# Sliding-window attention and a swish FFN on one core: two phases replaced by one planned graph of interleaved half batches

## The chip, the cores and the metric

The kernel runs on one core of a Trainium2 chip. The metric is the time of one execution on the device, in microseconds (us). Most executions of a kernel agree within about 1%. PE is the TensorE matmul engine, PEld its weight loads, DVE VectorE, ACT ScalarE, POOL GpSimd, SP the sync engine, whose queue issues most transfers. The "granted clock" is the share of PE's full speed that its throttle lets through. The traces record it only from 18 us on (before); the views count the unrecorded start as full clock. A run that is over 1.5% above the fastest of its kernel is called slow, and ratios use the other, fast runs alone.

## The reference

The inputs are float32. Attention with 4 sink tokens and a window of 128 is followed by a feed-forward network (FFN) with the activation h * sigmoid(beta * h).

```python
# q, k, v: (B=4, H=8, S=768, D=64); w_in (512, 2048); w_out (2048, 512); beta (2048,)
scores = q @ k.transpose(0, 1, 3, 2) / np.sqrt(D)
rel = pos[:, None] - pos[None, :]
keep = (pos[None, :] < 4) | ((rel >= 0) & (rel < 128))
a = softmax(np.where(keep, scores, -1e9))
x = (a @ v).transpose(0, 2, 1, 3).reshape(3072, 512)
h = x @ w_in
out = (h / (1 + np.exp(-beta * h))) @ w_out          # (3072, 512)
```

A block of 128 queries thus needs at most three blocks of 128 keys: its own (masked on the diagonal), the one before (masked the other way), and block 0, of which only the 4 sink keys count.

## The kernel before

There are two phases with a barrier between them. Phase A runs attention for the 16 pairs of heads, one pair after another. Each pair takes 12 transposes ahead of its scores, 30 score matmuls (contraction over 64 rows, the head dimension), six exps, six mask multiplications (two on GpSimd, four on DVE), and 30 AV matmuls. V carries a column of ones, so AV also gives the denominators. Every AV matmul contracts over 128 rows: for a sink block all 128 keys are multiplied, and the mask tile has set the exps of the other 124 to zero.

```python
# phase A, AV of one query block: all operands have 128 rows
lhsT = ET[:, e_idx, hh, j * 128:(j + 1) * 128]
rhs = v_aug[z][:, kb, hh, :]
te.matmul(out_ap, lhsT, rhs, start=(j == 0), stop=last)
...
# one pair after the other
for g in range(NPAIR):
    ...                                  # scores, exp, mask, AV of pair g
    epilogue_norm(g)
    transposes(g + 1)
    epilogue_trans(g)
    qk_copies(g + 1)
    epilogue_copy(g)
# phase B: 6 super-blocks of 512 tokens x 16 slices of d_ff
#   PE: 4 matmuls to hT (128x512); ACT: sig = sigmoid(beta * hT);
#   DVE: g = hT * sig; PE: 4 matmuls to the four output banks
```

The softmax here doesn't subtract the row's maximum and nothing guards it: scores larger than these inputs give would overflow.

## Time and profile before

The time is 329.79 us (median of three runs, 329.66 to 330.14).

| what | value | view |
|---|---|---|
| attention phase, up to the first FFN matmul | 153.6 us | timeline |
| mean granted clock there / afterwards | 0.66 / 0.99 | stretches |
| 128x512 matmul, start to start, full clock | 216 ns | matmul starts in the trace |
| 128-column transpose, start to start, half clock | 107 ns | same |
| one FFN super-block | 28.15 us | chain of waits |

First, lines of the page: busy time of each engine with its share of the span; then the span in 40 equal slices with the busy share in tenths (PEclk: granted clock in tenths).

```profile
PE 272.9 (83%) x2001; PEld 148.1 (45%) x2017; DVE 194.4 (59%) x329; ACT 141.2 (43%) x218; POOL 42.2 (13%) x52
...
PE   2577667766667688876999999999999999999994
...
PEclk9987576656775755575899999999999999999999
DMA  8999999999855576500000300030030002003003
```

Then the stretches before and after the first FFN matmul. The columns are the stretch, its length, busy time and number of instructions for PE, PEld, DVE, ACT and POOL, then granted clock, DMA share and GB/s.

```profile
0.00:153.60 153.60, 103.80 (x1250) 73.09 (x1251) 127.98 (x233) 63.14 (x98) 42.16 (x52) 0.66 0.79 179
153.60:329.00 175.40, 169.13 (x752) 75.06 (x766) 66.41 (x96) 78.09 (x121) 0.00 (x0) 0.99 0.10 37
```

The second phase is full of matmuls at full clock. In the first no engine is full: DVE is busiest (128 of 153.6 us), PE waits often and runs at half clock much of the time. The groups of instructions give the costs used below: line, engine, operation, tiles, shapes, count; busy us and mean ns of one; idle time just before, and what ended it.

```profile
L574 DVE TENSOR_TENSOR gsb<-hT,sig 128x512 bf16<-128x512 f32 x96 | 66.4, 692 | 103.9 <-PE oacc L595 92.0 <-ACT sig L566 11.9
L566 ACT ACTIVATE sig<-hT,beta_sb 128x512 bf16<-128x512 f32 x96 | 66.1, 689 | 92.8 <-PE hT L555 92.8
L354 PE MATMUL avout<-v_aug,ET 128*128 128x65 bf16 x480 | 40.9, 239 | 30.4 <-POOL ET L402 23.2 <-DVE ET L402 6.8
...
L393 ACT ACT_TABLE_LOAD x1 | 1.3, 1283 | 0.8 <-PEq L648 0.8
L566 ACT ACT_TABLE_LOAD x1 | 1.3, 1283 | 4.3 <-DVEq L500 4.3
```

The AV line (L354) gives a mean of 239 ns, which is the length of a pipelined matmul and not its cost. Its cost is the distance between starts, which is 54 ns here at half clock. The two table loads are one for exp and one for sigmoid.

### The profile page before, as it was taken

The numbers are of one execution on the slowest core, as the hardware profiler recorded it, in microseconds if no ns is written. First come the engines' busy times: TensorE is split into PE (matmuls) and PEld (weight loads), VectorE is DVE, ScalarE is ACT, GpSimd is POOL, SyncE is SP. The second block draws the span as 40 slices with busy tenths as digits, with TensorE's granted clock in tenths as the row PEclk, the third lists the DMA queues.
The fourth block names the chain that finished last, engine by engine and source line by source line (L and its number), as shares of the span: only waits on it lengthen the run. The fifth ranks groups of instructions, "written<-read, shape, count | busy, mean of one in ns | idle before, by whom it ended". The sixth has DMA issues, their size and how long they took to land.

```text
span 329.0 us, 5286 instructions
## 1 busy us (share of the span) xinstructions
PE 272.9 (83%) x2001; PEld 148.1 (45%) x2017; DVE 194.4 (59%) x329; ACT 141.2 (43%) x218; POOL 42.2 (13%) x52
## 2 busy tenths in 40 slices
PE   2577667766667688876999999999999999999994
PEld 1355445544444555553444444444444444444441
DVE  1687899999999999974344344334334334334331
ACT  1444443334444444443433633453453454445443
POOL 4222331123333222220000000000000000000000
PEclk9987576656775755575899999999999999999999
DMA  8999999999855576500000300030030002003003
GB/s 163 278 277 241 237 264 251 240 238 251 173 118 122 109 142 144 91 3 1 0 0 2 126 2 2 0 128 2 0 128 2 2 24 103 2 0 128 2 0 128
DMA packets 81465, 33.91 MB, mean 103 GB/s; under 512 B 75792, under 2 KB 75808, under 8 KB 80928
## 3 DMA queue, kind: packets, MB, share of 16 engines
q1 hardware_dynamic: 81440, 33.57, 41.8%
q8 instruction: 16, 0.26, 0.3%
q14 instruction: 9, 0.07, 0.1%
HBM read 27.27 MB, written 6.29 MB: 102 GB/s over the span
## 4 chain that ended last, share of the span: by engine, by line
PE 48%; issue 36%; POOL 10%; ACT 4%; DVE 1%; ACTq 0%; POOLq 0%; DVEq 0%
PE hT L555 24%; PE oacc L595 23%; POOL ET L402 9%; ACT outs L605 3%; POOL maskM L216 1%; ACT ET L393 1%; ACT sig L566 0%; DVE onorm L420 0%; PE avout L431 0%; PE avout L354 0%; DVE ET L402 0%; DVE xT L437 0%; ACTq L149 0%; POOL ident L216 0%; POOLq L50 0%
## 5 line engine op out<-in xcount | busy, mean ns | idle before, releaser
L574 DVE TENSOR_TENSOR gsb<-hT,sig 128x512 bf16<-128x512 f32 x96 | 66.4, 692 | 103.9 <-PE oacc L595 92.0
L566 ACT ACTIVATE sig<-hT,beta_sb 128x512 bf16<-128x512 f32 x96 | 66.1, 689 | 92.8 <-PE hT L555 92.8
L555 PE MATMUL hT<-xT,w_in 128*128 128x512 bf16 x376 | 99.5, 386 | 1.5 <-DVEq L500 1.1
L595 PE MATMUL oacc<-w_out,gsb 128*128 128x512 bf16 x376 | 99.0, 379 | 1.3
L393 ACT ACTIVATE ET<-score 128x768 bf16<-128x768 f32 (+1 forms) x96 | 61.5, 710 | 85.3 <-PE score L381 85.3
L354 PE MATMUL avout<-v_aug,ET 128*128 128x65 bf16 x480 | 40.9, 239 | 30.4 <-POOL ET L402 23.2
L595 PEld LDWEIGHTS oacc<-w_out,gsb 128*128 128x128 bf16 x384 | 37.5, 98 | 49.5 <-ACT outs L605 5.4
L555 PEld LDWEIGHTS hT<-xT,w_in 128*128 128x128 bf16 x384 | 38.1, 99 | 47.0 <-issue 2.8
L402 POOL TENSOR_TENSOR ET<-ET,maskM 128x256 bf16<-128x256 bf16 (+1 forms) x32 | 38.5, 1223 | 103.7 <-ACT ET L393 103.7
L354 PEld LDWEIGHTS avout<-v_aug,ET 128*128 128x128 bf16 x480 | 27.8, 122 | 47.0 <-POOL ET L402 30.0
L381 PE MATMUL score<-qkT 64*128 64x128 bf16 x480 | 31.8, 269 | 5.7 <-DVE qkT L322 3.2
L402 DVE TENSOR_TENSOR ET<-ET,maskM 128x768 bf16<-128x768 bf16 x64 | 32.1, 555 | 1.6 <-ACT ET L393 1.6
L381 PEld LDWEIGHTS score<-qkT 64*128 64x128 bf16 x480 | 17.9, 113 | 15.2 <-DVE qkT L322 8.4
L431 PE MATMUL avout<-ident,onorm 128*128 128x128 bf16 x96 | 12.2, 293 | 6.2 <-DVE onorm L420 6.2
L420 DVE TENSOR_TENSOR onorm<-avout,rden 128x384 bf16<-128x384 f32 x32 | 16.4, 552 | 0.6
L287 DVE CAST v_aug<-v_stage 128x768 bf16<-128x768 f32 x16 | 13.0, 814 | 3.6 <-DMA v_stage<-in_v_dram 3.6
L605 ACT ACTIVATE outs<-oacc 128x512 f32<-128x512 f32 x24 | 12.3, 604 | 1.4 <-PE oacc L595 1.4
L431 PEld LDWEIGHTS avout<-ident,onorm 128*128 128x128 bf16 x96 | 8.3, 130 | 10.3 <-DVE onorm L420 10.3
L437 DVE COPY xT<-avout 128x768 bf16<-128x768 bf16 x16 | 8.9, 556 | 0.9 <-PE avout L431 0.9
L320 DVE COPY qkT<-score 128x768 bf16<-128x768 bf16 x16 | 8.8, 548 | 0.0
L322 DVE COPY qkT<-score 128x768 bf16<-128x768 bf16 x16 | 8.8, 548 | 0.0
L409 DVE COPY den<-avout 128x12 f32<-128x12 f32 x16 | 2.7, 171 | 9.7 <-PE avout L354 9.7
(39 smaller groups left out, 99.9 us busy)
## 6 DMA issues: line engine op xcount, KB each, us to landing
q_stage<-in_q_dram SPq DMA_DIRECT2D x32, 192.0 KB, 4.6
k_stage<-in_k_dram SPq DMA_DIRECT2D x32, 192.0 KB, 4.9
v_stage<-in_v_dram SPq DMA_DIRECT2D x32, 192.0 KB, 4.1
out_dram<-outs SPq DMA_DIRECT2D x24, 256.0 KB, 2.3
w_in_stage<-in_moe_w_in_dram SPq DMA_DIRECT2D x4, 1024.0 KB, 6.8
w_out_stage<-in_moe_w_out_dram SPq DMA_DIRECT2D x4, 1024.0 KB, 7.5
beta_stage<-in_moe_beta_dram SPq DMA_DIRECT2D x1, 8.0 KB, 1.6
```

What stands on the lines that cost most here:

```text
L287: SD.op("dve", (lambda z: (lambda e: e.tensor_copy(v_aug[z][:, :, :, 0:D], v_stage[z][:, :, :, :])))(z), waits=[("vd%d" % z, 32 * nuse), ( ...
L354: (lambda te: te.matmul(out_ap, lhsT, rhs, start=(j == 0), stop=last)))
L381: (lambda te: te.matmul(out_ap, lhsT, rhs, start=True, stop=True)))
L393: (lambda e: e.activation(out_ap, in_ap, AF.Exp, bias=0.0, scale=SCALE)))
L402: (lambda e: e.tensor_tensor(out_ap, out_ap, mt, ALU.mult)))(out_ap, mt),
L420: (lambda e: e.tensor_tensor(dst, in0, in1, ALU.mult)))(dst, in0, in1),
L431: (lambda te: nc.tensor.transpose(out_ap, in_ap, ident[:, :])))(in_ap, out_ap),
L555: (lambda te: te.matmul(out_ap, lhsT, rhs, start=(c == 0), stop=last)))
L566: (lambda e: e.activation(sig_sb[i % NG][:, :], hT_ps[hb][:, 0:512], AF.Sigmoid, bias=0.0, scale=beta_sb[:, m:m + 1])))(i, m, hb),
L574: (lambda e: e.tensor_tensor(g_sb[i % NG][:, :], hT_ps[hb][:, 0:512], sig_sb[i % NG][:, :], ALU.mult)))(i, hb),
L595: (lambda te: te.matmul(out_ap, lhsT, rhs, start=(m == 0), stop=(m == NM - 1))))
L605: (lambda e: e.activation(out_sb[T % 2][:, t, :], out_acc[t][:, :], AF.Copy, bias=0.0, scale=1.0)))(T, t),
```

## The change

The intent is to fill PE's waits in attention with FFN matmuls, which have no dependence on the attention of later tokens. Everything becomes one graph. A planner in Python, with a small cost model, decides at build time in which order each engine gets its instructions; semaphores follow from the dependencies. The unit of attention is half a batch (3 query blocks) of one head pair. FFN super-blocks have 384 tokens, so that one needs just one half batch. Tanh replaces sigmoid: x*sigmoid(bx) = 0.5x(1 + tanh(bx/2)), the 0.5 folded into w_out. GpSimd masks each query block's own key block and the one before it with selects and does most casts of q, k and v. Of a sink block only the 4 sink keys are computed, as a 4-column score matmul and a 4-row AV matmul; so it needs no mask. (For the first two query blocks of a batch, block 0 is a window block too; it stays whole and is masked on DVE.)

The diff, cut to its core (removed phases and plumbing left out):

```diff
-        SD.op("act", ... e.activation(sig_sb[i % NG][:, :], hT_ps[hb][:, 0:512], AF.Sigmoid, ...
-        SD.op("dve", ... e.tensor_tensor(g_sb[i % NG][:, :], hT_ps[hb][:, 0:512], sig_sb[...], ALU.mult)
+        add("act", lambda e: e.activation(tt[ti][:, :], hp, AF.Tanh, bias=0.0, scale=hbeta[:, m:m + 1]), ...
+        add("dve", lambda e: e.scalar_tensor_tensor(gt[T_ % NG][:, m, :], tt[ti][:, :], 1.0, hp, ALU.add, ALU.mult), ...
...
+    GROUPS = [[[("s", 0, 0), ("s", 0, 1), ("d", 1, 1), ("p", 1, 2)], [("d", 2, 2), ("k", 0, 2)]],
+              [[("d", 3, 3), ("p", 2, 3), ("p", 3, 4)], [("d", 4, 4), ("d", 5, 5), ("p", 4, 5)],
+               [("k", 0, 3), ("k", 0, 4), ("k", 0, 5)]]]      # k: a sink block, 4 keys
...
+                dst = bank[0:NSINK if sink else 128, i0:i0 + st * (nq - 1) + 1:st, :]
+                lhsT = kt[rows, 1, 0:NSINK] if sink else kt[rows, 1, kc:kc + 128]
...
+                add("gp", ... e.affine_select(d, d, [[0, 2 * len(at_)], [sg, 128]], ALU.is_ge, 0.0, ...
...
+                    rows = slice(0, 128 if kb >= 0 else NSINK)          # AV
+                        e.matmul(A[:, c0:c0 + D + 1], E[z][rows, i, hh, :], vaug[vz][rows, kb % NK, 2 * hp + hh, :],
+                                 start=a, stop=o), mm_ns(D + 1), ...
...
+        for s in ("OT", "AV", "SC", "T") + ffn:     # planner: first head that is ready by now
+            h = head(s)
+            if h is None:
+                continue
+            if h[0] <= now:
+                best = (now, s, h[1])
+                break
```

## The prediction

> **What bounds the kernel now.** Two phases run one after the other. The timeline shows the first feed-forward (FFN) matmul at 153.6 us, after the last attention group. From there PE is the limit: the stretches from 160 us on are 98 to 99% PE at granted clock 1.00, the 128x512 matmuls start every 216 ns, a super-block takes 28.15 us. 768 x 216 ns = 166 us is that phase's floor; it takes about 175 us. The first 153 us are bound by no unit: one head pair takes 8 to 9.5 us in a serial loop. There DVE is 92% busy from 40 to 140 us, PE waits for GpSimd masks and DVE (the waits: 30.0 and 12.1 us), and the granted clock averages 0.66, so 128-column transposes start every 107 ns. The Trainium skill, "TensorE: Matmul & The Clock Gate", Part 1, says activity releases the half clock; the trace agrees (only 0.5 and 1.0 are granted; 1.0 throughout from 158 us).
>
> **What the change does.** FFN matmuls fill the attention's waits. PE work at full clock, from start-to-start times in the trace: FFN 166 us still (512 matmuls of 384 columns at about 162 ns, 384 of 512 at 216); transposes 288 x 56 ns = 16 us; scores: as many columns as before, the two heads' matmuls overlapping, about 14 us; AV 480 x about 42 ns = 20 us. Sum 216 us.
>
> Other engines, by estimate: ACT tanh 128 x 0.58 = 74 us, exp 65 us as before (61,440 columns), plus a share of copies; DVE g 128 x 0.56 = 71 us, normalisation 24 us, copies, masks and outputs 60 us, memsets 4 us. ACT and DVE together 300 us, 150 us each: below PE. GpSimd takes masks (about 55 us) and the q/k/v casts (about 41 us) at affine-select rates extrapolated from 292 ns for 128x128: about 100 us, off the limit, but it sets the pace of attention (13 us per half batch) until about 130 us. Tanh for sigmoid removes the second table load (1.28 us at 153.2 us): the skill's "ScalarE: Activation LUTs", Table sets, has exp and tanh in one set; the trace shows only that exp and sigmoid needed two.
>
> **Critical path.** Added to 216 us: the start. Half batch 0 (2.4 MB) lands by about 12 us, w_in by 28 us, half batch 1 by 37 us, w_out by 48 us at the 250 to 290 GB/s of the early slices; PE lacks work until then: about 35 us of work done at 50 us, so 15 us lost. Tail copy and store about 4 us. Waits where the planned order misjudges times, and half-clock windows while attention dominates: about 15 us, mostly before 130 us. Together 250 us.
>
> **Predicted: 250 us, 8 in 10 between 238 and 268 us. Faster by over 2%: 0.97, within 2%: 0.02, slower: 0.01.**
>
> **Right if:** one ACT table load; PE over 90% busy from 50 us to the end; granted clock 1.00 from 50 us but for a few windows; DMA input finished before about 130 us; ACT and DVE 55 to 70% busy, GpSimd 30 to 45%. Wrong if PE waits much on GpSimd masks, tanh or g.
>
> **What would make it wrong.** GpSimd selects slower than extrapolated (DVE colliding with it), so that attention stretches past 200 us; half clock persisting in the mixed stretch (up to 20 us more); fewer matmul stalls and faster loads than assumed (towards 238).

## The result, and the profile after

The changed kernel takes 288.92 us (median of four runs, 287.25 to 289.92) beside 329.97 us for the kernel before. The ratio is 0.8745 (95% interval 0.871 to 0.878). Ratios here are the mean time of one kernel's fast runs over that of the other's fast runs of the same rounds, so not quite the ratio of the medians. It is clearly faster, but the predicted range ended at 268 us.

The same lines of the page of the changed kernel:

```profile
PE 262.1 (92%) x1953; PEld 143.5 (50%) x1953; DVE 128.2 (45%) x252; ACT 172.4 (60%) x280; POOL 97.2 (34%) x192
...
PE   0249997989999999999999999999999999999995
...
PEclk9999999798999999999999999999999999999999
DMA  6962998899999997741000101010010101101001
```

And stretches of it, with the columns as above:

```profile
30.50:50.00 19.50, 17.42 (x134) 10.15 (x131) 13.03 (x23) 17.07 (x28) 9.84 (x16) 1.00 0.99 277
50.00:70.00 20.00, 19.00 (x124) 9.60 (x125) 9.68 (x19) 7.99 (x13) 12.22 (x19) 0.83 0.97 247
70.00:180.00 110.00, 109.96 (x1035) 62.84 (x1032) 53.48 (x116) 79.88 (x129) 65.91 (x129) 1.00 0.52 124
180.00:281.00 101.00, 100.49 (x548) 52.68 (x548) 41.15 (x75) 50.64 (x88) 0.00 (x0) 1.00 0.10 39
```

PE is full at full clock for 211 us on end (70 to 281 us), DVE is busy for 45% and ACT for 62% of that time, and the kernel is nevertheless 39 us later than predicted. So the loss is inside the time that counts as busy. The Trainium skill, "Trainium Kernel Development and Optimization", Performance Expectations, warns of just that: it calls matmul busy time a bad metric for the distance to the roofline. This trace agrees: experiment e1 below does the same sums 23 us sooner, and its PE is 99% busy too between 70 and 160 us:

```profile
70.00:160.00 90.00, 89.32 (x1020) 53.22 (x1019) 51.95 (x120) 78.28 (x126) 68.45 (x134) 1.00 0.66 159
```

The groups show one thing that was not there before: AV with 4 rows.

```profile
L517 PE MATMUL P<-vaug,E 128*128 128x65 bf16 x352 | 37.0, 204 | 0.0
...
L517 PE MATMUL P<-vaug,E 4*128 4x65 bf16 x128 | 25.7, 201 | 0.4 <-ACT E L474 0.4
...
L306 ACT ACT_TABLE_LOAD x1 | 1.3, 1283 | 3.3 <-DMA q_stage<-in_q_dram 3.3
```

Both kinds show about 200 ns each, so their length tells nothing. The timeline does: the 18 AV matmuls of one unit stand between an FFN group and the next one.

```profile
100.82 1.04 PE L573 MATMUL P<-w_out,g 128*128 128x512 bf16 x4
101.79 1.86 PE L517 MATMUL P<-vaug,E 4*128 4x65 bf16 x18
103.49 0.81 PE L555 MATMUL P<-xT,w_in 128*128 128x384 bf16 x4
```

They take 103.49 - 101.79 = 1.70 us, 94 ns each, at full clock, where 42 ns had been predicted. One by one, from the starts in the trace (contraction rows, then ns to the next start):

```
  4 -> 132   128 -> 38   128 -> 130
  4 -> 131   128 -> 39   128 -> 129
  4 -> 131   128 -> 39   128 -> 129
  4 -> 131   128 -> 38   128 -> 129
  4 -> 132   128 -> 38   128 -> 129
  4 -> 131   128 -> 39   128 -> 36 (an FFN matmul with 128 rows follows)
```

A 128-row AV matmul followed by another of its kind takes 38 ns. Before a 4-row one, and behind it, about 92 ns are added. The same addition stands wherever the number of contraction rows changes, in every kind of matmul that the table lists. Medians of the start-to-start distance, from 67 us to the end:

| matmul | same rows and columns next | other rows or columns next | difference |
|---|---|---|---|
| FFN, 512 columns | 216 ns | 312 ns (64 or 4 rows next) | 96 |
| FFN, 384 columns | 163 ns | 259 / 258 ns | 96 / 95 |
| transpose back, 128 columns | 56 ns | 151 ns | 95 |
| AV, 128 rows | 38 ns | 129 ns (4 rows next) | 91 |

The whole program has 355 changes of rows, 256 of them in and out of a 4-row AV matmul, and 31 changes of weight columns alone (between score matmuls with 128 and with 4 columns): 386 in all.

This gives the account below. Each start-to-start distance is put down to the earlier matmul; what exceeds 450 ns is counted as a gap.

| PE, us | predicted | changed kernel | e1 (no 4-row AV) |
|---|---|---|---|
| FFN | 166 | 173.6 | 171.8 |
| scores | 14 | 24.8 | 25.5 |
| transposes | 16 | 22.5 | 22.5 |
| AV | 20 | 43.4 | 19.3 |
| sum | 216 | 264.3 | 239.1 |
| before the first matmul, and gaps | 30 | 5.2 + 12.4 | 5.3 + 17.1 |
| after the last start | 4 | 3.5 | 3.6 |

The predicted losses for start and waits (30 us) were too high by 12, the matmul work too low by 48.

### The profile page after: what moved, and what is told of

It is laid out like the page before. It is cut to its first block, busy times and chain, and to the rows that moved or that the text cites. A ratio compares the mean times of both kernels' runs of the same rounds, so it can differ in the third digit from the quotient of the medians.

```text
span 285.5 us, 5121 instructions
## 1 busy us (share of the span) xinstructions
PE 262.1 (92%) x1953; PEld 143.5 (50%) x1953; DVE 128.2 (45%) x252; ACT 172.4 (60%) x280; POOL 97.2 (34%) x192
## 4 chain that ended last, share of the span: by engine, by line
PE 86%; ACT 4%; DMA 4%; SPq 2%; DVE 1%; issue 1%; POOL 0%; DVEq 0%
PE P L555 30%; PE P L573 30%; PE P L517 14%; PE P L467 6%; PE P L418 4%; DMA k_stage<-in_k_dram 3%; ACT E L474 2%; PE P L535 2%; SPq L349 2%; DMA q_stage<-in_q_dram 1%; ACT w_in L306 1%; DVE onorm L523 1%; ACT qkT L306 1%; ACT t L559 0%; DVE g L561 0%
## 5 line engine op out<-in xcount | busy, mean ns | idle before, releaser
L561 DVE SCALAR_TENSOR_TENSOR g<-t,P 128x384 bf16<-128x384 f32 x128 | 70.2, 554 | 94.0 <-ACT t L559 82.4
L559 ACT ACTIVATE t<-P,hbeta 128x384 f32<-128x384 f32 x128 | 73.8, 582 | 49.6 <-PE P L555 47.0
L555 PE MATMUL P<-xT,w_in 128*128 128x384 bf16 x512 | 100.8, 331 | 0.1
L573 PE MATMUL P<-w_out,g 128*128 128x512 bf16 x384 | 99.5, 385 | 0.5 <-DVE g L561 0.5
L474 ACT ACTIVATE E<-P 128x768 bf16<-128x768 f32 (+1 forms) x80 | 61.2, 817 | 19.3 <-PE P L467 19.2
L481 POOL TENSOR_SCALAR_AFFINE_SELECT E<-E 128x256 bf16<-128x256 bf16 (+1 forms) x112 | 54.7, 516 | 46.6 <-ACT E L474 46.6
L555 PEld LDWEIGHTS P<-xT,w_in 128*128 128x128 bf16 x512 | 48.5, 99 | 40.4 <-issue 4.6
L573 PEld LDWEIGHTS P<-w_out,g 128*128 128x128 bf16 x384 | 36.0, 99 | 36.3 <-issue 2.9
L517 PE MATMUL P<-vaug,E 128*128 128x65 bf16 (+1 forms) x480 | 46.5, 203 | 0.4 <-ACT E L474 0.4
L517 PEld LDWEIGHTS P<-vaug,E 128*128 128x128 bf16 (+1 forms) x480 | 31.6, 98 | 18.4 <-issue 3.2
```

What stands on the lines that cost most here:

```text
L474: add("act", lambda e: e.activation(dst_, src, AF.Exp, bias=0.0, scale=SCALE), act_ns(256 * n), w=[(k_, z, j) for k_ in "Edps"], x=[("B", ...
L481: add("gp", lambda e, d=d, sg=sg, at_=at_: e.affine_select(d, d, [[0, 2 * len(at_)], [sg, 128]], ALU.is_ge, 0.0, base=min(sg, 0), channel_ ...
L517: e.matmul(A[:, c0:c0 + D + 1], E[z][rows, i, hh, :], vaug[vz][rows, kb % NK, 2 * hp + hh, :], start=a, stop=o), mm_ns(D + 1),
L555: add("pe", lambda e, c=c: e.matmul(hp, w_in16[:, c, m * 128:(m + 1) * 128], xT[:, c, t0:t0 + HALF], start=(c == 0), stop=(c == 3)), mm_ns ...
L559: add("act", lambda e: e.activation(tt[ti][:, :], hp, AF.Tanh, bias=0.0, scale=hbeta[:, m:m + 1]), act_ns(HALF) + 93, r=["hbeta"], w=[("t" ...
L561: add("dve", lambda e: e.scalar_tensor_tensor(gt[T_ % NG][:, m, :], tt[ti][:, :], 1.0, hp, ALU.add, ALU.mult), dve_ns(HALF), r=[("t", ti)] ...
```

## The experiments

Theory A: each change of the row or column setting of PE costs about 92 ns, and the 4-row sinks make 256 of the 386 changes. Rival B: a 4-row matmul or its weight load is itself slow. Rival C: PE is held up because the planner's cost model is wrong. Rival D: GpSimd masks, or the start, set the time. All runs gave correct results. "Before" ran in the same rounds each time, 330.14 to 330.31 us median.

### e1: sinks over 128 rows

A tile vsink holds V's first 4 rows of a batch and zeros below, so contracting over all 128 rows adds nothing from the other keys, whatever finite numbers stand in E there.

```diff
+    vsink = sb("vsink", (128, H, D + 1), BF16, 2)        # zeroed once
+            add("gp", lambda e: e.tensor_copy(vsink[bp][0:NSINK, hs, :], vaug[hb % NV][0:NSINK, 0, hs, :]), ...
-                    rows = slice(0, 128 if kb >= 0 else NSINK)
-                        e.matmul(A[...], E[z][rows, i, hh, :], vaug[vz][rows, kb % NK, 2 * hp + hh, :], ...
+                    rhs = vsink[b % 2][:, 2 * hp + hh, :] if sink else vaug[vz][:, kb % NK, 2 * hp + hh, :]
+                        e.matmul(A[...], E[z][:, i, hh, :], rhs, ...
```

> AV's sink blocks contract over all 128 rows (a V copy that is zero below row 4) instead of over 4; right result. In the changed kernel's trace each of the 128 four-row matmuls has about 92 ns more than its neighbours in front of it and again behind it. Theory A (changing the row setting of the array costs about 92 ns each way): 256 changes x 92 ns = 23.5 us go; time about 265 us. Rival B (a 4-row weight load or matmul is itself slow, 130 in place of 40 ns): 128 x 90 = 11.5 us go; about 277 us. Rival C (PE waits because the planner misjudged times): no change, 287 to 290 us.

Measured: 265.75 us (264.44 to 267.08), ratio 0.8043 (0.801 to 0.8076); 23.2 us less than the changed kernel. Theory A had 265, B 277, C 289. The timeline of one unit, cut in the middle; it lasts from 94.00 us to 94.64 us, where the next group starts:

```profile
94.00 0.19 PE L527 MATMUL P<-vsink,E 128*128 128x65 bf16 x1
94.03 0.23 PE L527 MATMUL P<-vaug,E 128*128 128x65 bf16 x2
...
94.49 0.23 PE L527 MATMUL P<-vaug,E 128*128 128x65 bf16 x2
94.64 0.33 PE L476 MATMUL P<-qkT 64*4 64x384 bf16 x2
```

The 18 matmuls take 0.64 us in place of 1.70, 28 to 36 ns each, with one change at the end (121 ns).

### e2: the same matmuls in another order

```diff
+                if ps[0][3] < 0 and hh == 0:       # sink last in the first head's group,
+                    ps = ps[1:] + ps[:1]           # first in the second head's
+                elif ps[-1][3] < 0:
+                    ps = ps[-1:] + ps[:-1]
                 for n, (kind, j, i, kb) in enumerate(ps):
```

> Same matmuls, same shapes; only the order inside an accumulation group changes, so that sink matmuls of neighbouring groups stand next to each other: the number of changes between 4 and 128 rows falls from about 256 to about 128. Theory A: 128 x 92 ns = 11.8 us less, about 277 us. Rival B (the 4-row matmul itself is slow): no change, 289 us. Rival C: no change.

Measured: 275.44 us (274.32 to 276.86), ratio 0.8346 (0.8307 to 0.8385); 13.5 us less. In its trace exactly 128 changes in and out of 4 rows are left, and one unit of 18 takes 98.90 - 97.73 = 1.17 us:

```profile
97.73 1.33 PE L521 MATMUL P<-vaug,E 128*128 128x65 bf16 x18
98.90 0.81 PE L559 MATMUL P<-xT,w_in 128*128 128x384 bf16 x4
```

This is the cleanest test: every matmul and every shape is as in the changed kernel, only neighbours differ. Rivals B and C, which expected nothing, fall. The trace also settles B directly: a 4-row AV matmul followed by another 4-row one takes 39 ns to the next start, the same one followed by a 128-row one 124 ns (medians at full clock). Together e1 and e2 give 23.2 / 256 = 91 ns and 13.5 / 128 = 105 ns for one change, by the time of the whole kernel.

### e3: sink scores with all 128 key columns

```diff
-                dst = bank[0:NSINK if sink else 128, i0:i0 + st * (nq - 1) + 1:st, :]
-                lhsT = kt[rows, 1, 0:NSINK] if sink else kt[rows, 1, kc:kc + 128]
+                dst = bank[:, i0:i0 + st * (nq - 1) + 1:st, :]
+                lhsT = kt[rows, 1, kc:kc + 128]
```

> Sink scores use all 128 key columns as stationary operand in place of 4 (PE streams the same columns, exp and AV are as before); AV still contracts 4 rows. Theory A for columns: about 63 ns x 32 to 48 places, 2 to 3 us less, 286 us. If only the rows matter: no change, 288 to 289 us.

Measured: 286.32 us (median of the three fast runs, 285.44 to 287.96; the fourth was slow at 291.73), ratio 0.8673 (0.8634 to 0.8711), 2.6 us less by the medians of fast runs. That is what was expected, but the interval still touches that of the changed kernel (0.871 to 0.878). (The 1.8 us in e9's expectation below counts the slow run.) The trace is clearer: it has 31 changes fewer (355), and its score matmuls take 22.0 us from start to start in place of 24.8. In the changed kernel a score matmul with 128 columns followed by a 4-column one took 146 ns, and that case is gone. So a change of columns counts too, but only few of them stand here.

### e4: the first loads ahead of the first casts

In the changed kernel the k loads are issued on ACT's queue, and the planner put ACT's casts of q, which wait for q to land, between them. In the timeline of ACT's queue the last two k loads are issued from 11 us on.

```profile
4.21 0.49 ACTq L349 DMA_DIRECT2D k_stage<-in_k_dram  x1
4.55 0.52 ACT L306 ACTIVATE q_0<-q_stage 128x384 bf16<-128x384 f32 x1
...
9.40 0.92 ACTq L349 DMA_DIRECT2D k_stage<-in_k_dram  x2
...
11.05 1.88 ACTq L349 DMA_DIRECT2D k_stage<-in_k_dram  x2
```

```diff
-                if t is not None and ok and (t <= now + 500 or hb == 0):
+                if done["load"] >= 12 and t is not None and ok and (t <= now + 500 or hb == 0):
```

> The first half batch's loads are all queued before any cast is put on the engines' streams. In the changed kernel the k loads on ACT's queue stand behind ACT casts that wait for q, the last k landed at about 20 us and the first FFN matmul ran at 30.5 us. Theory: the start is serial and adds to the end one for one: first FFN matmul about 6 us earlier, time 281 to 284 us. Rival: the start is bound by the transfer rate, so nothing is gained (288 to 289 us).

Measured: 283.71 us (282.88 to 285.58), ratio 0.8594 (0.8557 to 0.863), 5.2 us less. All eight k loads now go out between 0.8 and 5.0 us:

```profile
0.80 4.24 ACTq L349 DMA_DIRECT2D k_stage<-in_k_dram  x8
```

The first FFN matmul starts at 24.3 us in place of 30.5. The start was serial and adds nearly one for one.

### e5: the planner is told what AV costs

```diff
-                                 start=a, stop=o), mm_ns(D + 1),
+                                 start=a, stop=o), 92,
```

> Only a number in the planner changes: an AV matmul is told to take 92 ns (its mean start-to-start time in the trace) in place of 30. Theory A: PE is full from 50 to 275 us whatever the order, so the time stays within 1% of 289 us. Rival C (the order is bad because the planner misjudges AV): 5 to 15 us less.

Measured: 295.08 us (293.85 to 297.37), ratio 0.8943 (0.889 to 0.8996): 6.2 us slower. Neither theory had this. It does show that a truer number in the cost model is not what was missing (rival C). The order differs: AV ends at 168 us in place of 181, and the third FFN super-block starts at 122 us in place of 99. The profiled run has 23.9 us in half-clock windows before its last matmul, against 6.8 us in the changed kernel. But a run of the changed kernel with a mean clock of 0.958, like this one's 0.959, took 289.85 us, so the clock alone does not explain it. Theory A's own expectation, that the time hardly depends on the order (within 1% of 289 us), failed here too. The cause stays open.

### e6: masks back on DVE

```diff
-                add("gp", lambda e, d=d, sg=sg, at_=at_: e.affine_select(d, d, ...
+                mk = maskD[:, i, :].unsqueeze(1).to_broadcast([128, 2 * len(at_), 128])
+                add("dve", lambda e, d=d, mk=mk: e.tensor_tensor(d, d, mk, ALU.mult), ...
```

> The window masks go from GpSimd selects to DVE multiplications by a mask tile (undoing that part of the change). GpSimd loses 55 us of work, DVE gains about 45 us. If PE is the limit: within 1% of 289 us, at most 2 us off either way. If GpSimd sets the pace of attention, and that matters: several us less.

Measured: 287.33 us in its one fast run; the other three were slow runs at 292.33 to 292.89 us, which are not compared. DVE went from 128.2 to 160.3 us busy, GpSimd from 97.2 to 56.6 (the profile is of a slow run; the work did move). The fast run lies at the lower end of the changed kernel's runs. One run is no verdict, but nothing says that GpSimd's masks held the kernel up or gained it time.

### e7: sigmoid again

```diff
-        ... AF.Tanh, bias=0.0, scale=hbeta[:, m:m + 1]) ; (t + 1) * h ; 0.5 in w_out and hbeta
+        ... AF.Sigmoid, bias=0.0, scale=hbeta[:, m:m + 1]) ; h * t ; factor 1.0 in both
```

> Tanh goes back to sigmoid, everything else stays interleaved. On ACT's stream exp and tanh alternate 61 times, so about 61 more table loads of 1.28 us: 78 us more on ACT (172 to about 250 us of 285). If ACT then holds attention and FFN back while both run: 310 to 340 us. If ACT's slack hides all of it: 289 us.

Measured: 342.75 us (341.20 to 345.61), ratio 1.0388 (1.0333 to 1.0442): slower than the kernel before. The groups of table loads:

```profile
L559 ACT ACT_TABLE_LOAD x31 | 39.8, 1283 | 0.5
L474 ACT ACT_TABLE_LOAD x30 | 38.5, 1283 | 0.5
```

These are 61 loads of 1.28 us more than with tanh, 78 us of ACT, and the time is 54 us longer. Half of that is PE standing still (gaps of 41.4 us in place of 12.4); the rest is matmuls further apart, with 58.0 us of half-clock windows in place of 6.8. The Trainium skill, "ScalarE: Activation LUTs", Table sets: the hidden batching unit, lists exp and tanh in one set and sigmoid's as another; this trace agrees, with one load in the whole changed kernel. In the two-phase kernel, with two loads in all, tanh would save one. In this interleaved order it saves 61, and with sigmoid the interleaving loses to the kernel before. Sigmoid with e1's sinks, or in an order that alternates less, was not run.

### e8 and e12: all FFN after all attention

```diff
-            h = head(s)
+            h = head(s) if s not in "HO" or done["OT"] == NU else None
```

> The same program, but no FFN block is taken before the last attention unit is done, so the interleaving alone is undone. Attention alone would be set by loads and GpSimd (about 97 us of work after a start of 20 us), ending at 120 to 130 us; then the FFN needs 166 us and a tail of 4: 290 to 305 us. If so, interleaving is worth only 1 to 15 us, because the mixed stretch has only about 50 us of PE idle to fill. If interleaving is what makes the change: 320 us or more.

> e8 (FFN after all attention) with e1's 128-row sinks. In e8 the attention took 165 us at half clock, PE 85 to 90% busy, and a change between 4 and 128 rows costs about 115 ns there. If PE is what bounds attention alone: up to 256 x 0.115 = 29 us less than e8's 339.9, about 315 us. If loads and GpSimd bound it: 335 to 340 us.

Measured: e8 339.90 us (338.19 to 341.98), ratio 1.0294 (1.0246 to 1.0343); e12, with e1's sinks, 316.41 us (315.13 to 319.52), ratio 0.9588 (0.9526 to 0.9651). The expectation of 290 to 305 us for e8 was wrong. The page of e8:

```profile
PE   0474188498889889998799999999999999999996
...
PEclk9999995555557675585599999999999999999999
```

The first FFN matmul starts at 165.5 us, and until then the clock is at half most of the time, as in the kernel before. The attention matmuls' start-to-start distances add up to 127 us (91 us in the changed kernel). Attention alone is thus not set by loads and GpSimd alone, but to a good part by PE at half clock and with changes of rows: e12, without the 256 changes, is 23.5 us faster than e8. Not all of that need be the changes themselves, for the half-clock windows shrank as well, from 102 to 55 us in the profiled runs, while the gaps grew from 33.8 to 44.5 us. The Trainium skill, "TensorE: Matmul & The Clock Gate", Part 1, says that the half clock is the default and that activity releases it. These traces agree in part: the same attention matmuls run at 1.00 when FFN matmuls stand among them (70 to 180 us in the changed kernel). But in e8 PE looks busy at half clock too:

```profile
90.00:100.00 10.00, 8.99 (x72) 5.22 (x72) 2.04 (x6) 4.34 (x7) 7.43 (x15) 0.50 1.01 229
```

Interleaving is worth 339.90 - 288.92 = 51.0 us with the 4-row sinks and 316.41 - 265.75 = 50.7 us without. Filled waits are the smaller part of it: from e8 to the changed kernel PE's gaps shrink by 21 us (33.8 to 12.4), the time of the attention's own matmuls by 36 us (127 to 91), with half-clock windows of 7 us in place of 102, while FFN matmuls take 5 us more.

### e9, e10, e11: the parts together

e9 is e1, e3 and e4 in one kernel. e10 also moves the second half batch's loads ahead of the third weight block; e11 also takes score groups in a row.

```diff
-    LOADS = xl(0) + [0, 1, 2, 3] + xl(1) + [4, 5, 6, 7] + ...
+    LOADS = xl(0) + [0, 1] + xl(1) + [2, 3, 4, 5, 6, 7] + ...                    # e10, e11
+        while s == "SC":                                                          # e11
+            h = head("SC")
+            if h is None or h[0] > G.free["pe"] + 100:
+                break
+            h[1]()
+            done["SC"] += 1
```

> e1, e3 and e4 together. If they add: 288.9 - 23.2 - 1.8 - 5.2 = 258.7 us, a range of 256 to 262. If the start's gain is hidden once PE has less to do (attention then waits for loads and GpSimd between 40 and 70 us): 262 to 265 us.

> As e9, and the second half batch's loads stand before the third block of w_in on the sync queue. There that queue was blocked from 10 to 21 us (29 us in the changed kernel) by a weight staging buffer, and the transfers fell to about 110 GB/s. If the stretch to 70 us is bound by loads: 3 to 6 us less than e9. If not: the same as e9.

> As e10, and the planner takes the next score group at once after one when it is ready within 100 ns, so that fewer changes between 64 and 128 rows stand in the order. If each change costs 92 ns: up to 2 us less than e10; less if waiting groups were adjacent already.

Measured: e9 255.08 us (253.57 to 255.58), ratio 0.7711 (0.7681 to 0.7741). e10 256.01 us (254.48 to 256.50), ratio 0.7739 (0.7707 to 0.7771). e11 257.58 us (256.79 to 258.13), ratio 0.7794 (0.7765 to 0.7823). The three parts add up and a little more (33.8 us against 23.2 + 2.6 + 5.2 = 31.0); e9 beats both kernels. The page of e9 has no low slice in PEclk any more, which may be the rest (not shown):

```profile
PE   1477997699999999998999999999999999999994
...
PEclk9999999999999999999999999999999999999999
```

e10 and e11 gain nothing. In their profiled runs 104 changes are left, in e9 100 (each of these traces lacks 26 to 28 matmul records): no sign that e11's rule removed any. e10's order does not help the stretch to 60 us: by then 103 FFN matmuls have started, 117 in e9.

## Why the prediction was right or wrong

- "What bounds the kernel now": right. Attention leaves PE waiting at half clock, the FFN runs at PE's rate.
- "FFN matmuls fill the attention's waits": right, but not the whole of it. e8 shows that interleaving is worth 51 us, and the larger part is attention matmuls that start closer together, with far less half clock, and not filled waits.
- "PE work at full clock ... Sum 216 us": this is the step that failed. The sum took streaming costs of matmuls next to their like and left out what stands between unlike ones. Measured: 264.3 us; 386 changes at about 93 ns are 36 of the missing 48 us. The largest term is "AV 480 x about 42 ns = 20 us", which was 43.4 us; e1 brings it to 19.3 us by taking away the row changes alone. "Scores ... about 14 us" was 24.8 us (81 of the changes follow score matmuls, about 7.5 us; the rest was not taken apart), "transposes 288 x 56 ns = 16 us" 22.5 us (the first ones, before the clock was recorded, started every 107 ns, as they do in half-clock windows, and 23 changes cost about 2.6 us), "FFN 166 us" 173.6 us (2.8 us at changes, 2.4 us in half-clock windows).
- The evidence was there. The diff shows the 4-row operands. The trace of before has AV matmuls followed by 64-row score matmuls at a median of 130 ns at full clock (176 at half), against 38 ns (54 at half) between AV matmuls. And the Trainium skill, "TensorEngine Tiling (Array Packing)", Key Properties, says "Mode switching requires drain". The traces here fit that and give it a size, 91 to 96 ns at full clock; that the added time is a drain they do not show. With 386 changes, counted from the changed kernel's trace, 386 x 93 ns = 36 us by this estimate. That this is nearly the 39 us by which the prediction was short is partly luck: the work was 48 us more, and 12 us of overestimated losses hid a part of that.
- "The start ... 15 lost" and "about 15 us" of waits: too high together. Gaps were 5.2 + 12.4 us in place of 30; half-clock windows, which the 15 us were to hold too, are counted with the work above. e4 shows that 5.2 us of the start could be had back.
- "Tanh for sigmoid removes the second table load": right, and far too small a view of it: in the interleaved order 61 loads would stand there (e7).
- "GpSimd ... sets the pace of attention ... until about 130 us": wrong. AV ends at 181 us. Input transfers did end by about 130 us, GpSimd was 34% busy. PE itself set the pace: it was busy without a break from 70 to 180 us, and e1, with less PE work, ends AV at 161 us.
- "PE over 90% busy from 50 us to the end; granted clock 1.00 from 50 us but for a few windows": both came true, and the time was still 39 us off. They could not tell a right sum from a wrong one, because the time added at the changes counts as busy. ACT at 60% was within the range given, DVE at 45% below it.

## What to carry to other kernels

Cost a stream of matmuls by the distance between starts, and look at it separately where neighbours differ in contraction rows or weight columns: on this core each such change cost about 92 ns, more than twice a 65-column matmul. A small operand that saves mask work on an engine with slack can cost more on the one without; pad it with zeros to its neighbours' shape, or put like next to like. When work of different kinds is interleaved, check that it shares one activation table, and don't accept "PE is busy at full clock" as proof that a sum of PE work is right.

## What the Trainium skill lacked or had wrong

- "TensorEngine Tiling (Array Packing)", Key Properties, says that a mode switch drains PE, but gives no size, and its section When to Use Tiling offers row tiling for contractions of 64 or less without naming this cost. Here: 91 to 96 ns for each change at full clock (216 to 312 ns, 163 to 259 ns, 38 to 129 ns), and about 122 ns at half clock in the kernel before (54 to 176 ns).
- "TensorE: Matmul & The Clock Gate", Back-to-back issue gap, gives a sustained 131 ns for 512 columns and 81 ns for 128 in real streams of weight loads and matmuls. Here such streams start every 216 ns and 56 ns at full clock, which is its isolated figure; 65 columns went at 28 to 39 ns.
- No page gives the time of GpSimd's affine selects. Here 128x256 bf16 took 446 ns, 128x512 bf16 693 ns, and a 128x512 cast from float32 by a select 612 to 679 ns in the group means.
- "TensorE: Matmul & The Clock Gate", Part 1, ties the clock to how busy PE is, but the busy share that a profile shows is no guide to it: in e8 PE was 86% busy from 50 to 160 us (mean of the ten-microsecond stretches) at granted clocks of 0.50 to 0.76.
